# Tile 0's last column group as seven products of quarters, with a copy on VectorE, an earlier q packing and a later table load

## The chip, the cores and the metric

The kernel runs on one core of a Trainium2 chip. The core has five engines with a queue of instructions each: TensorE (PE in the profile; its weight loads are shown apart, as PEld), VectorE (DVE), ScalarE (ACT), GpSimd (POOL) and SyncE (SP). Every engine runs its own queue in order, and they meet through semaphores. Loads from main memory go over 16 DMA engines; nearly all of them are issued from POOL's queue here, the stores and the transposing DMAs from SP's.

The metric is the time of the kernel on the device, in microseconds (us), from the first instruction to the end. A profiled execution also has a span, from its first to its last recorded instruction.

## The reference

```python
def _attn_ref(q, k, v, g_norm):                      # (8, 8, 576, 64) each
    kv = np.einsum('bhsd,bhse->bhde', k, v)
    out = np.einsum('bhsd,bhde->bhse', q, kv)
    rms = np.sqrt(np.mean(out * out, axis=-1, keepdims=True) + 1e-06)
    return (out / rms * g_norm).astype(np.float32)

def _moe_ref(x, w_in, w_out):                        # (4608, 512), (512, 2048), (2048, 512)
    h = x @ w_in
    g = h * (1.0 / (1.0 + np.exp(-1.702 * h)))
    return (g @ w_out).astype(np.float32)
```

The attention's output, with its heads joined to rows of 512, is the second part's x.

## The kernel before

The 4608 rows are done in nine tiles of 512. Tile t (0 to 7) holds the first 512 rows of batch t; the ninth collects the 64 rows that are left over from each batch. For a tile the kernel needs the attention of its batch (transposed, as xT: four chunks `ko` of 128 model columns by 512 rows), then the "hidden" products (h = x @ w_in, as 16 column groups `fo` of 128), a gate on ScalarE (`gT`), and the projection with w_out.

Tiles 1 to 8 compute both matrix products with seven products of quarters instead of eight (Winograd's form of Strassen's scheme). For the hidden part, a group g (`PARTS` = 0, 2, 4, 6) covers columns i, i+1 and i+8, i+9. `SevenIn.product(p)` issues the four 256-wide matmuls of product p. The sums of weights (`ws`, made by `w_in_sums`) and of activations (`xS`, made by `Sums.form`) are made on VectorE. Products 1, 6, 7 and 4 accumulate one after another in one PSUM bank, "x". After product 1 that bank is copied to a bank "y", where product 2 adds to it (`snap[1]` names the engine, A for ScalarE, D for VectorE). Product 5 goes to a bank "z" and is copied to SBUF as `s5` (`snap[5]`). Once 5 and 6 are there, VectorE puts x + s5 into z, to which product 3 adds; after 7 it puts x + s5 into s5; 4 adds to x. The four results are gated from y, z, x and s5. So a product of the "x" bank may not start before VectorE has read what the one before it left there.

Tile 0 is done plainly: each column is four matmuls of 512 (`Hidden.mm`, line 487) and a gate (`Hidden.gate`, line 496). Columns 0 to 3 and 8, 9 run while batch 0's attention ends (lines 895 to 913); `first_columns` does the ten others in the order of `COLS`. Then `project_all` issues the 64 projection matmuls of tile 0 as steps n = 0 to 63: a row group `mo` (of four) and a column `fo` each. Between them, at step numbers given by hand, stand the units of batch 1's attention: `q` (transposes of q on TensorE, copied by ScalarE), `kv`, `out`, `ss` and `apply`. `at1(i, ...)` hangs a unit behind column i of `first_columns`, `at2(n, ...)` behind step n of the projection.

What VectorE does beside that in tile 0: it scales w_in by the norm's weights for the later tiles (`scale_w_in`, line 207; tile 0 has them in its x instead, and so uses w_in before it is scaled), makes the sums of w_in (lines 509 to 512) and of w_out (`weight_sum`, line 622), packs batch 1's q (`pack_q`, line 420), clears `kvd` (line 982), casts kv to `kvb` (line 385), and applies the roots (line 370).

The order on each engine is the order in which the Python code records it (`manual_schedule`); the framework adds the waits and hands out PSUM banks: `ps_a` and `ps_h` have three, `ps_o` has two.

Of the kernel before, what the change touches and what calls it, by code (L numbers as in the profile page):

```python
# [16 lines left out]
def kernel(  # L17
# [10 lines left out]
    nc = tc.nc  # L28

    B, H, S, D = q.shape  # L30
# [3 lines left out]
    FO = DFF // P  # L34
# [8 lines left out]
    PE_ = 96  # L43
    NJ = S // PE_
    GROUP = 6
    COLS = (0, 1, 2, 3, 8, 9, 10, 11, 4, 5, 6, 12, 13, 7, 14, 15)
    assert PE_ * NJ == S and PE_ % 32 == 0

    const = ctx.enter_context(tc.tile_pool(name="const", bufs=1))
# [15 lines left out]
    kvd = [const.tile([P, NPAIR, 2, 2, D], F16, name=f"kvd{i}") for i in range(2)]  # L65
# [15 lines left out]
    PARTS = range(0, HF, 2)  # L81
# [61 lines left out]
    for n in "kqv":  # L143
# [13 lines left out]
        out=ident,  # L157
# [340 lines left out]
    def quarters(w, f, k):  # L498

        hi = slice(HF * P + f.start, HF * P + f.stop)  # L500
        lower = slice(KH + k.start, KH + k.stop)
        return w[:, k, f], w[:, lower, f], w[:, k, hi], w[:, lower, hi]

    def w_in_sums(g0, g1):

        f = slice(2 * g0 * P, 2 * g1 * P)
        a11, a12, a21, a22 = quarters(w_in_sb, f, slice(0, KH))
        s = [ws[:, n, :, f] for n in range(4)]
        nc.vector.tensor_add(s[0], a21, a22)
        nc.vector.tensor_sub(s[1], s[0], a11)  # L510
        nc.vector.tensor_sub(s[2], a11, a21)
        nc.vector.tensor_sub(s[3], a12, s[1])

    class Sums:

# [27 lines left out]
    def copy(engine, to, src):  # L543
        (nc.vector.tensor_copy if engine == "D" else nc.scalar.copy)(to, src)  # L544
# [244 lines left out]
    def layers(t, units1, units2):  # L789
        hid = d0 if t == 0 else Hidden(t)  # L790
        seven = Seven(t, hid.gT) if t else None
        left = hid_seven(t, hid, seven, units1) if t else first_columns(hid, units1)
        osbs[t] = opool.tile([P, 4, DM], F32, name="osb", tag="osb")
        if t:
            todo = {n: [lambda x=x: seven.sums(*x) for x in xs] for n, xs in plan(t).later.items()}
            for n, us in units2.items():
                todo.setdefault(n, []).extend(us)
            for n, us in left.items():
                todo[n] = us + todo.get(n, [])
            seven.run(todo)  # L800
        else:
            project_all(hid.gT, units2)
        if t < B and t not in HALVED:
            store(t, 0, J)

    def first_columns(hid, units):

        for i, fo in enumerate(COLS):
            if i >= GROUP:
                for ko in range(KO):  # L810
                    hid.mm(ko, fo)
                hid.gate(fo)
            for u in units.get(i, ()):
                u()

    def project_all(gT, units):

        os = {}

        def project(mo, fo):  # L820
            if fo == 0:
                pool, tag = (ps_h, "hT") if mo < 2 else (ps_o, "o")
                os[mo] = pool.tile([P, DM], F32, name="o", tag=tag)
            nc.tensor.matmul(  # L824
                os[mo],
                gT[:, fo, mo * P : (mo + 1) * P],
                w_out_sb[:, fo, :],
                start=(fo == 0),
                stop=(fo == FO - 1),
            )  # L830
            if fo == FO - 1:
                copy = nc.scalar.copy if mo % 2 else nc.vector.tensor_copy
                copy(osbs[0][:, mo, :], os[mo])

        steps = [(mo, f + k) for f in (0, 4) for mo in range(4) for k in range(4)]
        steps += [(mo, f + k) for f in range(8, FO, 2) for mo in range(4) for k in range(2)]
        for n, (mo, fo) in enumerate(steps):
            project(mo, fo)
            for u in units.get(n, ()):
                u()  # L840

    def store(t, j0, j1):
        nc.sync.dma_start(
            out=out[t * S : t * S + SM, :].rearrange("(p j) m -> p j m", j=J)[:, j0:j1],
            in_=osbs[t][:, j0:j1],
        )
# [58 lines left out]
    for fo in range(4):  # L905
        d0.mm(2, fo)
    for fo in COLS[0:4]:
        d0.mm(KO - 1, fo)
        d0.gate(fo)
    for fo in COLS[4:GROUP]:  # L910
        for ko in range(KO):
# [13 lines left out]

    made = {}
    osbs = {}
    SECOND = Plan(
# [38 lines left out]
    def plan(t):  # L967
        return SECOND if t < EARLY else LATER if t < B - 1 else LAST_TWO

# [7 lines left out]
    for t in range(NT):  # L977
        b = t + 1
        u1, u2 = {}, {}

        def at1(i, f, *args):
            u1.setdefault(i, []).append(lambda: f(*args))

        def at2(i, f, *args):
            u2.setdefault(i, []).append(lambda: f(*args))  # L985

        def of(b, name, *args):
            return lambda: getattr(live[b], name)(*args)

        if t == 0:  # L990
            for l in range(2):
                at1(6, nc.vector.memset, kvd[l], 0.0)
            at1(7, scale_w_in, 0, 4)
            at1(7, w_in_sums, 0, 2)
            at1(8, start, 1)
            at1(12, scale_w_in, 4, 6)
            at1(12, w_in_sums, 2, 3)
            at1(13, load_q, 2)
            at2(4, nc.scalar.preload_act_table_set, "abs_reciprocal_sqrt_and_small")
            at2(18, weight_sum, 0, 0, HF)  # L1000
            at2(18, scale_w_in, 6, 8)
            at2(18, w_in_sums, 3, 4)
            for c in range(NPAIR):
                at1(12, of(1, "pack_q", c))
                at2(9 + 3 * c, of(1, "q", c))
                at2((38, 39, 51, 51)[c], of(1, "kv", c))
                at2((43, 45, 55, 56)[c], of(1, "out", c))
                at2((47, 50, 59, 61)[c], of(1, "ss", c))
                at2((49, 53, 59, 62)[c], of(1, "apply", c))
            for n in range(1, 4):  # L1010
                at2(19, weight_sum, n, 0, 2)
                at2(40, weight_sum, n, 2, 6)
            at2(39, load_kv, 2, 0, H // 2, False)
            at2(51, clear_rest)
            at2(51, load_kv, 2, H // 2, H)

            def first_sum():
                made[1] = Sums(1, xT[1])
                made[1].form(0)

            at2(55, first_sum)
        elif b < B:
            todo = plan(t)
            at1(todo.steps.index("kv"), of(b, "kv_all", todo.keep))
            if t == 1:
                at1(5, start, b)
                at1(5, of(b, "transpose_q"))
                at1(4, nc.scalar.preload_act_table_set, "gelu_apprx_sigmoid_and_others")
                for n, i in ((1, 8), (2, 11), (3, 16)):
                    at1(i, weight_sum, n, 6, HF)  # L1030
            if t + 2 < B:
                late = max(15, todo.steps.index("kv") + 1)
                at1(late, load_kv, t + 2)
                at1(late, load_q, t + 2)
                at2(100, start, t + 2)
                at2(100, of(t + 2, "transpose_q"))
            if t == B - 2:
                for early in range(EARLY):
                    at1(20, load_q_rest, early, qre[early])
                at2(100, rests.transpose)  # L1040
            at = todo.attn
            at2(at["table"], nc.scalar.preload_act_table_set, "abs_reciprocal_sqrt_and_small")
            for h in range(2):
                at2(at["roots"][h], of(b, "roots", h))
            for j in range(J):
                for name in ("rows", "add_up", "turn"):
                    at2(at[name][j], of(b, name, j))
            at2(46, of(b, "out", NPAIR))
            at2(74, of(b, "ss", NPAIR))
            at2(80, of(b, "apply", NPAIR))  # L1050
            at2(82, nc.scalar.preload_act_table_set, "gelu_apprx_sigmoid_and_others")
        elif t < B:
            at2(16, rests.out)
            at2(34, nc.scalar.preload_act_table_set, "abs_reciprocal_sqrt_and_small")
            at2(44, rests.ss)
            at2(50, rests.apply)
            at2(52, nc.scalar.preload_act_table_set, "gelu_apprx_sigmoid_and_others")
        layers(t, u1, u2)


# [28 lines left out]
```

## Time and profile before

| | us |
|---|---|
| three runs | 261.21, 263.64, 263.35 |
| their median | 263.35 |
| the profiled execution | 261.35 |
| its span | 259.6 |

The page of the profile gives, for each engine, its busy time, share of the span and number of instructions. A line of an instruction group names the line of the kernel, the engine, the operation, the tile written and the tiles read with their shapes, how often it ran; after the bar busy time and mean ns of one; after the second bar the idle time in front of them and what ended it. In a timeline a line begins with start and duration in us, and ends, in square brackets, with the engine's idle time before it and who released it. Matmuls overlap in the array: a matmul's busy time is longer than the distance from its start to the next one's.

### The profile page before, as it was taken

What the parts mean: (1) busy time and instruction counts of PE and PEld (TensorE: products, weight loads), DVE (VectorE), ACT (ScalarE), POOL (GpSimd) and SP (SyncE); (2) the same over time, 40 slices, a digit from 0 to 9 for tenths busy, and PEclk for the clock granted to TensorE, in tenths of its full rate; (3) what the DMA queues carried; (4) which work ended last, traced back from release to release, by engine and by line L of the source; (5) the groups of instructions that cost most, each with busy time, mean ns of one, the idle gap of its engine ahead of it and who ended that gap; (6) DMA issues with size and microseconds to landing.
All of it is one profiled execution on the core that took longest, in us unless ns stands there. A gap on an engine that the chain in (4) does not pass through costs nothing.

```text
span 259.6 us, 6081 instructions
## 1 busy us (share of the span) xinstructions
PE 252.1 (97%) x2475; PEld 205.9 (79%) x2475; DVE 194.2 (75%) x350; ACT 174.1 (67%) x313; POOL 56.3 (22%) x85
## 2 busy tenths in 40 slices
PE   8899999999999999999999999999999999999992
PEld 2434544788888988899889888988899889888882
DVE  1656658999968986898689968995899578467931
ACT  2487715988649964996499649964897569737810
POOL 8962335116034003500250017200000000000000
PEclk9999999999999999999999999999999999999999
DMA  8999999999999976994799969998601520021005
GB/s 171 186 202 204 203 203 196 246 162 154 179 166 139 225 107 162 159 204 68 169 65 222 148 159 130 232 99 144 153 3 27 149 91 3 0 110 54 4 0 162
DMA packets 69886, 35.42 MB, mean 136 GB/s; under 512 B 39330, under 2 KB 67746, under 8 KB 69602
## 3 DMA queue, kind: packets, MB, share of 16 engines
q0 software_dynamic: 39056, 18.19, 56.2%
q1 hardware_dynamic: 30480, 16.45, 29.6%
q8 instruction: 19, 0.31, 0.5%
q10 hardware_dynamic: 322, 0.39, 0.5%
q14 instruction: 9, 0.07, 0.1%
HBM read 36.70 MB, written 9.44 MB: 178 GB/s over the span
## 4 chain that ended last, share of the span: by engine, by line
PE 92%; POOL 3%; DMA 2%; ACT 1%; DVE 1%; issue 0%
PE h L594 38%; PE o L716 38%; PE o L824 5%; PE hT L487 5%; DMA w_in_sb<-in_moe_w_in_dram 2%; PE outR L308 2%; PE kvp L236 2%; POOL qraw L99 1%; PE ss L356 1%; POOL kraw L101 1%; POOL vbuf L101 1%; ACT rs L358 1%; PE kvp L248 0%; PE outT L281 0%; PE q L429 0%; DVE xT L366 0%
## 5 line engine op out<-in xcount | busy, mean ns | idle before, releaser
L574 ACT ACTIVATE gT<-h 128x512 f16<-128x512 f32 x96 | 52.8, 604 | 5.4 <-PE h L594 5.4
L594 PEld LDWEIGHTS <-ws 128*128 128x128 f16 x512 | 50.1, 98 | 6.0
L716 PEld LDWEIGHTS <-gS 128*128 128x128 f16 x512 | 49.7, 98 | 5.8
L594 PE MATMUL h<-xS,ws 128*128 128x256 f16 x384 | 52.2, 273 | 0.0
L716 PE MATMUL o<-tw,gS 128*128 128x256 f16 x384 | 46.4, 273 | 0.0
L594 PEld LDWEIGHTS <-w_in_sb 128*128 128x128 f16 x384 | 37.1, 98 | 4.8
L716 PEld LDWEIGHTS <-gT 128*128 128x128 f16 x384 | 37.0, 98 | 4.0
L716 PE MATMUL o<-w_out_sb,gT 128*128 128x256 f16 x256 | 33.5, 273 | 0.0
L594 PE MATMUL h<-xT,w_in_sb 128*128 128x256 f16 x224 | 31.9, 273 | 0.0
L691 DVE TENSOR_TENSOR osb<-o,qf 128x512 f32<-128x512 f32 (+1 forms) x25 | 16.7, 668 | 14.7 <-PE o L716 11.9
L608 DVE TENSOR_TENSOR h<-h,s 128x512 f32<-128x512 f32 x32 | 22.2, 697 | 6.7 <-PE h L594 5.5
L113 POOL DMA_DIRECT2D kraw<-in_k_dram x7 | 6.0, 854 | 92.7 <-PE kvp L236 87.4
L610 DVE TENSOR_TENSOR s<-h,s 128x512 f32<-128x512 f32 x32 | 22.1, 691 | 4.1 <-PE h L594 3.3
L646 DVE TENSOR_TENSOR gS<-gT 128x512 f16<-128x512 f16 (+2 forms) x32 | 21.6, 684 | 0.6 <-ACT gT L574 0.6
L574 ACT ACTIVATE gT<-s 128x512 f16<-128x512 f32 x32 | 19.8, 628 | 2.6 <-DVE s L610 2.6
L985 ACT ACT_TABLE_LOAD x15 | 19.2, 1283 | 0.3
L745 POOL DMA_DIRECT2D out_dram<-osb x2 | 1.1, 559 | 84.3 <-DVE osb L691 84.3
L358 ACT ACTIVATE rs<-ss,eps_t 128x512 f32<-128x512 f32 (+1 forms) x14 | 8.2, 597 | 16.0 <-PE ss L356 15.9
L594 PE MATMUL h<-xS,w_in_sb 128*128 128x256 f16 x128 | 18.9, 273 | 0.0
L544 ACT COPY h<-h 128x512 f32<-128x512 f32 x27 | 15.7, 587 | 2.1 <-PE h L594 2.0
L594 PE MATMUL h<-xT,ws 128*128 128x256 f16 x112 | 16.8, 273 | 0.0
L544 ACT COPY s<-h 128x512 f32<-128x512 f32 x18 | 10.6, 589 | 8.8 <-PE h L594 8.2
(105 smaller groups left out, 373.3 us busy)
## 6 DMA issues: line engine op xcount, KB each, us to landing
out_dram<-osb SPq DMA_DIRECT2D x12, 512.0 KB, 3.0
kraw<-in_k_dram POOLq DMA_DIRECT2D x5, 512.0 KB, 8.2
vbuf<-in_v_dram POOLq DMA_DIRECT2D x5, 512.0 KB, 11.8
qraw<-in_q_dram POOLq DMA_DIRECT2D x4, 512.0 KB, 14.4
out_dram<-osb SPq DMA_DIRECT2D x2, 1024.0 KB, 5.6
qbuf<-in_q_dram POOLq DMA_DIRECT2D x3, 512.0 KB, 12.8
w_in_sb<-in_moe_w_in_dram POOLq DMA_DIRECT2D x2, 512.0 KB, 10.5
w_out_sb<-in_moe_w_out_dram POOLq DMA_DIRECT2D x2, 512.0 KB, 14.8
```

Source lines behind the costliest of these rows:

```text
L358: nc.scalar.activation(rs[:, 0:n], t[:, 0:n], AFT.Abs_reciprocal_sqrt, bias=eps_t, scale=1.0 / D)
L487: nc.tensor.matmul(self.h[fo], w_in_sb[:, ko, fo * P : (fo + 1) * P], self.x[:, ko], start=(ko == 0), stop=(ko == KO - 1),)
L544: (nc.vector.tensor_copy if engine == "D" else nc.scalar.copy)(to, src)
L574: nc.scalar.activation(self.gT[:, to, n * TH : (n + 1) * TH], src, AFT.Gelu_apprx_sigmoid)
L594: nc.tensor.matmul(bank[name][:, a], w, x, start=(p in (1, 5) and a == 0 and k == 0), stop=(k == KH - 1), skip_group_check=True,)
L608: nc.vector.tensor_add(bank["z"], bank["x"], self.s5)
L610: nc.vector.tensor_add(self.s5, bank["x"], self.s5)
L646: op(s[:, n, lo], a, b)
L691: nc.vector.tensor_add(o, ps, self.kept[with_][:, m])
L716: nc.tensor.matmul(o, a, w, start=(p in (1, 2, 5) and i == 0 and (mo == 0 or split)), stop=(i == HF - 1), skip_group_check=True,)
L824: nc.tensor.matmul(os[mo], gT[:, fo, mo * P : (mo + 1) * P], w_out_sb[:, fo, :], start=(fo == 0), stop=(fo == FO - 1),)
L985: u2.setdefault(i, []).append(lambda: f(*args))
```

## The change

Columns 6, 7, 14 and 15 of tile 0 (group 3) are computed with the seven products. `COLS` keeps the six early columns, and `COLS_LATER` lists the others, in which a string is a product: column 10, 11, 4, product 1, column 5, product 2, columns 12 and 13, products 5, 6 and 7. Products 3 and 4 stand in the projection, behind steps 3 and 7. The plan `FIRST` says that product 1 is copied by ScalarE and product 5 by VectorE. The sums of x are made behind column 10, group 3's sums of the unscaled w_in behind column 13; behind step 19 of the projection that part of w_in is scaled and summed again for the later tiles.

Beside it, the first scaling and the sums of w_in move to other places, `kvd` is cleared by GpSimd, the packing of q hangs behind step 0 of the projection and not behind column 13, with the q load for tile 2 behind step 8, and ScalarE's table of roots is loaded behind step 20, not step 4. The attention's units from `kv` on stand one or two steps later, both units of a kv pair at one step, and the last eight projection steps go through the row groups in the order 2, 0, 3, 1.

```diff
-    COLS = (0, 1, 2, 3, 8, 9, 10, 11, 4, 5, 6, 12, 13, 7, 14, 15)
+    COLS = (0, 1, 2, 3, 8, 9)
+    COLS_LATER = (10, 11, 4, "1", 5, "2", 12, 13, "5", "6", "7")
...
-    def w_in_sums(g0, g1):
+    def w_in_sums(g0, g1, which=range(4)):
...
         else:
+            for n, us in left.items():
+                units2[n] = us + units2.get(n, [])
             project_all(hid.gT, units2)
...
     def first_columns(hid, units):
 
-        for i, fo in enumerate(COLS):
-            if i >= GROUP:
+
+        xs = Sums(0, hid.x)
+        part = SevenIn(hid, xs, len(PARTS) - 1, FIRST)
+        gates = []
+        for i, fo in enumerate(COLS_LATER):
+            if isinstance(fo, str):
+                gate = part.product(int(fo))
+                if gate:
+                    gates.append(gate)
+            else:
                 for ko in range(KO):
                     hid.mm(ko, fo)
                 hid.gate(fo)
+            if fo == 5 or fo == 12:
+                while gates:
+                    gates.pop()()
+            if i == 0:
+                for n in range(4):
+                    xs.form(n)
             for u in units.get(i, ()):
                 u()
+
+        def late(p):
+            gates.append(part.product(p))
+            gates.pop()()
+            while p == 4 and gates:
+                gates.pop()()
+
+        return {3: [lambda: late(3)], 7: [lambda: late(4)]}
...
             if fo == FO - 1:
-                copy = nc.scalar.copy if mo % 2 else nc.vector.tensor_copy
+                copy = nc.vector.tensor_copy if mo in (2, 0) else nc.scalar.copy
                 copy(osbs[0][:, mo, :], os[mo])
 
         steps = [(mo, f + k) for f in (0, 4) for mo in range(4) for k in range(4)]
-        steps += [(mo, f + k) for f in range(8, FO, 2) for mo in range(4) for k in range(2)]
+        steps += [(mo, f + k) for f in (8, 10, 12) for mo in range(4) for k in range(2)]
+        steps += [(mo, 14 + k) for mo in (2, 0, 3, 1) for k in range(2)]
...
+    FIRST = Plan("", {}, {}, {1: "AAAA", 5: "DDDD"}, "D", "aaaa", "aaaa", {}, ())
...
             for l in range(2):
-                at1(6, nc.vector.memset, kvd[l], 0.0)
-            at1(7, scale_w_in, 0, 4)
-            at1(7, w_in_sums, 0, 2)
-            at1(8, start, 1)
-            at1(12, scale_w_in, 4, 6)
-            at1(12, w_in_sums, 2, 3)
-            at1(13, load_q, 2)
-            at2(4, nc.scalar.preload_act_table_set, "abs_reciprocal_sqrt_and_small")
+                at1(0, nc.gpsimd.memset, kvd[l], 0.0)
+            at1(1, scale_w_in, 0, 4)
+            at1(1, w_in_sums, 0, 2, (0, 1))
+            at1(2, start, 1)
+            at1(7, w_in_sums, 3, 4)
+            at2(1, w_in_sums, 0, 2, (2, 3))
+            at2(8, scale_w_in, 4, 6)
+            at2(8, w_in_sums, 2, 3)
+            at2(8, load_q, 2)
+            at2(20, nc.scalar.preload_act_table_set, "abs_reciprocal_sqrt_and_small")
             at2(18, weight_sum, 0, 0, HF)
-            at2(18, scale_w_in, 6, 8)
-            at2(18, w_in_sums, 3, 4)
+            at2(19, scale_w_in, 6, 8)
+            at2(19, w_in_sums, 3, 4)
             for c in range(NPAIR):
-                at1(12, of(1, "pack_q", c))
+                at2(0, of(1, "pack_q", c))
                 at2(9 + 3 * c, of(1, "q", c))
-                at2((38, 39, 51, 51)[c], of(1, "kv", c))
-                at2((43, 45, 55, 56)[c], of(1, "out", c))
-                at2((47, 50, 59, 61)[c], of(1, "ss", c))
-                at2((49, 53, 59, 62)[c], of(1, "apply", c))
+                at2((39, 39, 53, 53)[c], of(1, "kv", c))
+                at2((44, 46, 56, 57)[c], of(1, "out", c))
+                at2((48, 51, 60, 62)[c], of(1, "ss", c))
+                at2((50, 54, 60, 63)[c], of(1, "apply", c))
...
             at2(39, load_kv, 2, 0, H // 2, False)
-            at2(51, clear_rest)
-            at2(51, load_kv, 2, H // 2, H)
+            at2(53, clear_rest)
+            at2(53, load_kv, 2, H // 2, H)
```

More of the change, by code (lines that the diff above doesn't have):

```diff
@@ L508, in w_in_sums @@
         s = [ws[:, n, :, f] for n in range(4)]
[L509 to L512, printed above, removed]
+        for n in which:
+            op, a, b = (
+                (nc.vector.tensor_add, a21, a22),
+                (nc.vector.tensor_sub, s[0], a11),
+                (nc.vector.tensor_sub, a11, a21),
+                (nc.vector.tensor_sub, a12, s[1]),
+            )[n]
+            op(s[n], a, b)
     class Sums:
```

## The prediction

> **What bounds the kernel now.** I read the busy table first, then the chain of waits, then a table of stages.
>
> ```profile
> PE 252.1 (97%) x2475; PEld 205.9 (79%) x2475; DVE 194.2 (75%) x350; ACT 174.1 (67%) x313; POOL 56.3 (22%) x85
> PE 92%; POOL 3%; DMA 2%; ACT 1%; DVE 1%; issue 0%
> 17.00:28.27 11.27, 11.22 (x52) 5.07 (x52) 7.59 (x14) 8.94 (x16) 3.51 (x5) 1.00 1.30 204
> 28.27:46.60 18.33, 18.18 (x137) 8.75 (x136) 11.63 (x28) 9.08 (x15) 7.93 (x11) 1.00 1.35 200
> 46.60:73.50 26.90, 26.90 (x288) 23.69 (x287) 24.85 (x45) 20.70 (x37) 5.26 (x7) 1.00 1.24 178
> ```
>
> TensorE (PE) is busy 97% of the span and carries 92% of the chain that ended last. The last three rows are tile 0's columns, tile 0's projection (with batch 1's attention), and tile 1; columns are length, then busy time of PE, weight loads, VectorE (DVE), ScalarE (ACT), GpSimd (POOL), the granted clock (1.00), DMA. PE has no pause in tile 1, so a microsecond won or lost in tile 0 reaches the end whole. Busy hides short stalls behind modelled tails; I therefore work with start times.
>
> **The columns: less work, two new waits.**
>
> ```profile
> 17.05 11.38 PE L487 MATMUL hT<-xT,w_in_sb 128*128 128x512 f16 x52 [0.27 <-DVE xT L366]
> 28.27 2.32 PE L824 MATMUL o<-w_out_sb,gT 128*128 128x512 f16 x10
> 75.12 11.02 PE h L594 x100
> L594 PEld LDWEIGHTS <-ws 128*128 128x128 f16 x512 | 50.1, 98 | 6.0
> ```
>
> From the first row's start to the second's, 52 matmuls of 512 columns take 11.22, so 0.2158 each. The third (the chain in order of time) gives 0.110 for one of 256. The change drops four columns, 16 x 0.2158 = 3.45, and adds 28 x 0.110 = 3.08: 0.37 us less PE work. The weight loads, 98 ns in the fourth row, still fit under 110.
>
> [...]
>
> What a product waits for:
>
> ```profile
> 17.53 3.77 ACT L496 ACTIVATE gT<-hT 128x512 f16<-128x512 f32 x7
> 22.43 0.60 ACT L496 ACTIVATE gT<-hT 128x512 f16<-128x512 f32 x1 [0.27 <-PE hT L487]
> 47.43 0.61 ACT L544 COPY h<-h 128x512 f32<-128x512 f32 x1
> 21.57 0.87 DVE L207 TENSOR_SCALAR w_in_sb<-w_in_sb,g_col 128x2048 f16<-128x2048 f16 x1 [2.70 <-PE hT L487]
> 22.48 0.69 DVE L509 TENSOR_TENSOR ws<-w_in_sb 128x1024 f16<-128x1024 f16 x1
> 23.81 0.68 DVE L511 TENSOR_TENSOR ws<-w_in_sb 128x1024 f16<-128x1024 f16 x1
> 23.83 0.72 POOL L195 DMA_DIRECT2D w_out_sb<-in_moe_w_out_dram  x1 [1.88 <-DMA w_in_sb<-in_moe_w_in_dram]
> 26.41 0.42 DVE L509 TENSOR_TENSOR ws<-w_in_sb 128x512 f16<-128x512 f16 x1
> ...
> 27.54 0.42 DVE L512 TENSOR_TENSOR ws<-w_in_sb,ws 128x512 f16<-128x512 f16 x1
> 49.14 0.69 DVE L544 COPY s<-h 128x512 f32<-128x512 f32 x1
> L608 DVE TENSOR_TENSOR h<-h,s 128x512 f32<-128x512 f32 x32 | 22.2, 697 | 6.7 <-PE h L594 5.5
> ```
>
> Column 10 starts at 17.05 + 12 x 0.2158 = 19.64, before and after. Then 10, 11 and 4 end issuing at 22.23, "1" at 22.67, column 5 at 23.53. "2" adds into a bank that ACT copies from "1". ACT gates column 4 from 22.43 and, at its pitch of 0.54 (3.77 for seven), copies from about 22.97 for 0.61: PE waits until about 23.63, 0.1 lost. "2" ends at 24.07; the weights of columns 12 to 15 have landed by 23.83, where POOL's issue was released by them; 12 and 13 end at 25.80. "5" needs the first w_in sum of the group. DVE's scaling still waits for column 11 and two sums follow as in the rows, so the new 0.42 sums start near 23.85 and the first is ready near 24.3: hidden. The four x sums (0.42 each) sit in DVE's 2.70 of waiting.
>
> The third wait is not hidden. "5" ends at 26.24, "6" at 26.68, and "7" accumulates into the very bank that DVE must still read for z = x + s5 (the add behind "6"); that add needs the copy s5 of "5". A 512 matmul shows 0.38 busy at 0.216 spacing, so results stand about 0.16 after issue ends: 26.40. DVE copies 26.45 to 27.14 (0.69), adds to about 27.87 (0.70 by the last row), and "7" starts at 27.90 instead of 26.68: 1.22 us of idle PE, with the whole projection queued behind it. In tile 1 other products stand between these three; here nothing does. "7" ends at 28.34, where the projection began at 28.27. "3" and "4" follow inside the projection, 0.88 together; the second add (done near 29.25) comes before "4" at 30.5. So step 8 starts at 30.95, against 28.27 + 8 x 0.2158 = 30.00. Sum: -0.37 + 0.10 + 1.22 = +0.95.
>
> **Moves beside PE.**
>
> ```profile
> 28.73 1.03 DVE L420 COPY qbuf<-qraw 128x512 f16<-128x512 f16 x4 [0.77 <-DMA qraw<-in_q_dram]
> 31.33 1.23 DVE L622 TENSOR_TENSOR tw<-w_out_sb 128x2048 f16<-128x2048 f16 x1 [1.58 <-DMA w_out_sb<-in_moe_w_out_dram]
> 32.47 0.87 DVE L207 TENSOR_SCALAR w_in_sb<-w_in_sb,g_col 128x1024 f16<-128x1024 f16 x2
> 38.73 0.59 DVE L385 CAST kvb<-kvp 64x128 f16<-64x128 f32 x2 [2.79 <-PE kvp L248]
> 39.91 1.24 ACT L299 ACTIVATE sq<-outT 128x512 f16<-128x512 f32 x2 [5.86 <-PE outT L281]
> 17.06 1.02 DVE L982 MEMSET kvd<- 128x512 uint32 x2
> 1.26 0.20 POOL L165 MEMSET ones<- 128x128 f16 x1
> 33.25 0.91 POOL L131 DMA_DIRECT2D qraw<-in_q_dram  x1 [1.02 <-DVE w_in_sb L207]
> 48.38 6.38 SPq L271 DMA_TRANSPOSE qTd<-qraw  x1
> 59.64 0.39 PE L308 MATMUL outR<-kvd,qTd 128*128 128x128 f16 x4
> ```
>
> The packing of q, though recorded sooner, now stands behind the second add and starts at about 29.25, not 28.73; its first reader, q's transpose after step 9, comes near 31.2: nothing. DVE's queue up to the kvb casts is then packing 1.03, two sums of 0.69, two scalings of pairs 0.87, eight small w_in sums at 0.39 (the four from 26.41 to 27.96; the group's sums are made twice now, unscaled and scaled), 1.23, and three weight sums of that size: 9.7 us, to 38.95. The casts come due at 38.73 + 0.95 - 0.15 = 39.5. Nothing, but 0.6 is all that covers it. The table load (one, behind the last gate and the four q copies, by 36) lies in ACT's 5.86 of idle. The memsets move to POOL, in front of tile 2's q load (33.25) with its two rest loads and the kv loads behind it. No row shows POOL clearing such a tile: DVE's 1.02 for both is the lower bound, and POOL's 0.20 for an eighth as many columns, times sixteen, 3.2, the upper; I take 2, between them. The q load feeds SP's transpose at 48.38, first read at 59.64; 2 us vanish there.
>
> **The projection's end.**
>
> ```profile
> 40.78 0.38 PE L356 MATMUL ss<-sq,ones 128*128 128x512 f16 x1
> 41.20 0.69 ACT L358 ACTIVATE rs<-ss,eps_t 128x512 f32<-128x512 f32 x1
> 41.94 0.38 PE L356 MATMUL ss<-sq,ones 128*128 128x512 f16 x1
> 42.46 0.57 PE L248 MATMUL kvp<-vbuf,kraw 96*64 96x64 f16 x24
> 42.96 1.04 PE L824 MATMUL o<-w_out_sb,gT 128*128 128x512 f16 x4
> 43.84 0.38 PE L281 MATMUL outT<-qT,kvb 128*128 128x512 f16 x1
> 45.13 0.38 PE L356 MATMUL ss<-sq,ones 128*128 128x512 f16 x1
> 45.97 0.38 PE L356 MATMUL ss<-sq,ones 128*128 128x512 f16 x1
> 46.61 0.60 PE L594 MATMUL h<-xT,w_in_sb 128*128 128x256 f16 x4
> ```
>
> The attention units sit one or two steps later. The two kv groups become one run and save about 0.15. The second kv pair leaves three steps (0.65) instead of four (0.86) before the product that needs its cast, which can start 0.88 after kv's last matmul was issued (42.96 to 43.84): 0.2 lost. The last ss goes into the bank of the one before; it waits for that root: from ss to ss 0.38 + 0.04 + 0.69 + 0.05 = 1.16, as between the first two before (40.78 to 41.94), where 45.13 to 45.97 was 0.84. That is 0.3 lost. Together +0.35; bounds -0.4 (every present pause gone) and +0.7.
>
> Total +1.3. The profiled execution took 261.35 us (span 259.6 and 1.75 around it) and would take 262.65; the median of the runs, 263.35, is 2.0 above it and becomes **264.6**.
>
> **Rivals.** First, product 7's wait is no wait of consequence, because DVE answers faster or PE's order hides it, and the saved 0.37 stands together with up to 0.4 of removed pauses: 262.6 to 263.0, faster. For: the work does fall. Against: the 0.69 and 0.70 rows, and nothing queued between.
>
> Second, slower by more than 1%: DVE becomes late at the kvb casts. Its place is the queue priced at 9.7 us with 0.6 of cover; POOL's clearing runs in the same stretch as DVE's scalings and sums. What DVE loses there beyond 0.6 us, PE waits for at the casts; 2 us lost gives 1.3 + 1.4 = 2.7, hence 266.0, and from 1.9 on it passes 1%. For: the 2.79 of idle ahead of the casts is used up. Against: the packing alone can slip freely. [...]
>
> Third, weight loads set the pace of the seven products. If a product matmul cost 0.123 (3.45 / 28) nothing would be saved: 265.0. Against it: 100 of them at 0.110.
>
> **Numbers.** Chances: forecast 0.68, first rival 0.12, second 0.14, third 0.03, the rest 0.03. A measurement of this kernel tells about 1% from no change. The forecast (+0.5%) and the first rival lie within 1%; the second is beyond. So slower 0.16, same 0.80, faster 0.04, the last for runs that fall near 261.2 on one side and 263.6 on the other, as the three shown do. The range: from 262.65, the sum on the profiled execution, less 0.65 for the tail's lower bound, 262.0; to the highest run, 263.64 + 1.3 + 0.85 for the tail's upper bound and POOL, 265.8.
>
> **What would show it.** Right: a pause of about 1.2 us before the third group of "h" products from xS in tile 0, with DVE's copy and add in it back to back; step 8 about 0.95 later; tile 1 starting near 47.9. Wrong: that pause under 0.5; kvb casts that start with no wait for PE (DVE late); or tile 1 starting before 46.6.

## The result, and the profile after

| | kernel before | changed kernel |
|---|---|---|
| median of 22 runs each, us | 261.68 | 262.52 |
| lowest and highest, us | 261.21, 263.64 | 262.16, 262.94 |
| the profiled execution, us | 261.35 | 262.91 |
| its span, us | 259.6 | 261.1 |

The ratio of the changed kernel to the one before is 1.0027 (95% interval 1.0016 to 1.0038): 0.7 us slower by the ratio, 0.84 by the medians. The forecast was 264.6 us, or 1.3 us slower than a base of 263.35; the range of 262.0 to 265.8 holds the time. The direction is right, the size is not, and the base is off by more than the change. Of 85 further runs of the kernel before, made beside the experiments, the three above 263 us had a mean granted clock of 0.989 and the other 82 one of 0.995 to 1.000; for 263.64 and 263.35 no clock is on record.

The page of the changed kernel: busy time of PE and the others, the engines' shares of the chain, and the group of products with a sum as operand (after the second bar the idle time in front of them).

```profile
PE 251.7 (96%) x2487; PEld 206.9 (79%) x2487; DVE 198.1 (76%) x359; ACT 174.2 (67%) x314; POOL 58.7 (22%) x87
...
PE 90%; POOL 3%; DMA 3%; DVE 1%; ACT 1%; issue 0%; DVEq 0%
...
L599 PE MATMUL h<-xS,ws 128*128 128x256 f16 x396 | 53.9, 273 | 1.2 <-DVE h L613 1.2
```

PE has 12 matmuls more and 0.4 us less busy time, yet the span is 1.5 longer. The group that had no idle time before now has 1.2 us of it in one place, ended by VectorE's addition. The stages of the changed kernel, cut at the same times as those of before (length, then busy time of PE, weight loads, DVE, ACT, POOL, the granted clock, DMA):

```profile
17.00:28.27 11.27, 9.88 (x52) 4.99 (x52) 7.13 (x15) 8.22 (x15) 3.87 (x5) 1.00 1.30 204
28.27:46.60 18.33, 18.04 (x143) 9.28 (x143) 14.74 (x35) 8.51 (x14) 8.80 (x12) 1.00 1.35 200
46.60:73.50 26.90, 26.56 (x280) 22.90 (x278) 25.25 (x47) 22.23 (x40) 6.33 (x9) 1.00 1.24 174
```

The clock is 1.00 as before. The first pauses stand in the columns: 11.27 - 9.88 = 1.39 us without PE, where it was 0.05. The timeline of that place:

```profile
18.40 4.49 PE L488 MATMUL hT<-xT,w_in_sb 128*128 128x512 f16 x20 [0.22 <-DMA w_in_sb<-in_moe_w_in_dram]
...
26.22 1.04 PE L599 MATMUL h<-xS,ws 128*128 128x256 f16 x8
26.86 0.69 DVE L549 COPY s<-h 128x512 f32<-128x512 f32 x1 [1.03 <-PE h L599]
27.68 0.70 DVE L613 TENSOR_TENSOR h<-h,s 128x512 f32<-128x512 f32 x1
28.44 0.60 PE L599 MATMUL h<-xS,ws 128*128 128x256 f16 x4 [1.18 <-DVE h L613]
31.47 0.59 PE L853 MATMUL o<-w_out_sb,gT 128*128 128x512 f16 x2
```

The row at 26.22 is products 5 and 6, together 8 x 0.110 = 0.88 of issue, to 27.10. Then VectorE copies, adds, and product 7 starts at 28.44: 1.34 us in which PE issues nothing, with copy and add back to back. (The row counts 1.18 of idle: the eight matmuls' busy time of 1.04 reaches 0.16 past their 0.88 of issue.) The first row belongs to this execution alone: a matmul waited for a transfer of w_in. A second profile of the same kernel, in the experiments, doesn't have that wait, and is compared with the kernel before here:

```profile
22.37 0.60 PE L599 MATMUL h<-xT,w_in_sb 128*128 128x256 f16 x4
...
28.08 0.60 PE L599 MATMUL h<-xS,ws 128*128 128x256 f16 x4 [1.18 <-DVE h L613]
31.11 0.59 PE L853 MATMUL o<-w_out_sb,gT 128*128 128x512 f16 x2
...
47.50 0.38 PE L357 MATMUL ss<-sq,ones 128*128 128x512 f16 x1 [0.34 <-ACT rs L359]
47.93 0.60 PE L599 MATMUL h<-xT,w_in_sb 128*128 128x256 f16 x4
```

Product 1 starts at 22.37; the 24 matmuls of 0.2158 in front of it put the start of that row at 17.19, where the kernel before has 17.05. From there step 8 of the projection (31.11) is 13.92 away; before, it was 30.00 - 17.05 = 12.95. From step 8 to tile 1 (47.93) it is 16.82, before 46.61 - 30.00 = 16.61. So the columns and the two late products cost 0.97 us, and the rest of the projection 0.21. What tile 1 does with it is in the chain of waits, in order of time. The kernel before:

```profile
46.78 9.44 PE h L594 x84
56.21 0.75 PE kvp L236 x40
```

and the changed kernel's second profile:

```profile
48.10 9.17 PE h L599 x84
57.27 0.75 PE kvp L237 x40
```

The same 84 matmuls take 9.17 and not 9.44: tile 1 gives back 0.27. Together 0.97 + 0.21 - 0.27 = 0.91, and 0.14 for the start; the two profiled executions are 262.45 - 261.35 = 1.10 apart. Where the 0.27 was in the kernel before, its timeline shows:

```profile
46.97 0.59 ACT L833 COPY osb<-o 128x512 f32<-128x512 f32 x1
47.05 0.60 PE L594 MATMUL h<-xS,ws 128*128 128x256 f16 x4
...
47.61 0.60 PE L594 MATMUL h<-xT,w_in_sb 128*128 128x256 f16 x4
...
50.25 0.60 PE L594 MATMUL h<-xT,w_in_sb 128*128 128x256 f16 x4
50.81 1.03 PE L594 MATMUL h<-xS,ws 128*128 128x256 f16 x8
```

Four matmuls take 0.44 from start to start; here it is twice 0.56. PE counted as busy through both, since the modelled end of a matmul (0.60 after the group's start) covers the gap. The group at 47.61 starts 0.05 after ScalarE has ended a copy of an accumulator (46.97 + 0.59 = 47.56). That this copy held it back is a reading, on which one of the experiments below rests.

### The profile page after: what moved, and what is told of

The parts are those of the page before. It is cut to its first block, busy times and chain, and to the rows that moved or that the text cites. A ratio compares the mean times of both kernels' runs of the same rounds, so it can differ in the third digit from the quotient of the medians.

```text
span 261.1 us, 6119 instructions
## 1 busy us (share of the span) xinstructions
PE 251.7 (96%) x2487; PEld 206.9 (79%) x2487; DVE 198.1 (76%) x359; ACT 174.2 (67%) x314; POOL 58.7 (22%) x87
## 3 DMA queue, kind: packets, MB, share of 16 engines
HBM read 36.70 MB, written 9.44 MB: 177 GB/s over the span
## 4 chain that ended last, share of the span: by engine, by line
PE 90%; POOL 3%; DMA 3%; DVE 1%; ACT 1%; issue 0%; DVEq 0%
PE h L599 39%; PE o L721 37%; PE o L853 5%; DMA w_in_sb<-in_moe_w_in_dram 3%; PE hT L488 3%; PE outR L309 2%; PE kvp L237 2%; POOL qraw L100 1%; POOL kraw L102 1%; POOL vbuf L102 1%; PE ss L357 1%; POOL w_in_sb L171 1%; ACT rs L359 1%; PE kvp L249 0%; PE outT L282 0%; PE q L430 0%
## 5 line engine op out<-in xcount | busy, mean ns | idle before, releaser
L579 ACT ACTIVATE gT<-h 128x512 f16<-128x512 f32 x99 | 54.5, 604 | 9.3 <-PE h L599 9.3
L599 PEld LDWEIGHTS <-ws 128*128 128x128 f16 x528 | 51.7, 98 | 7.7 <-issue 1.4
L599 PE MATMUL h<-xS,ws 128*128 128x256 f16 x396 | 53.9, 273 | 1.2 <-DVE h L613 1.2
L599 PEld LDWEIGHTS <-w_in_sb 128*128 128x128 f16 x396 | 38.3, 98 | 5.5 <-issue 0.2
L599 PE MATMUL h<-xT,w_in_sb 128*128 128x256 f16 x232 | 33.1, 273 | 0.0
L613 DVE TENSOR_TENSOR h<-h,s 128x512 f32<-128x512 f32 x33 | 23.0, 698 | 6.9 <-PE h L599 5.5
L615 DVE TENSOR_TENSOR s<-h,s 128x512 f32<-128x512 f32 x33 | 22.8, 691 | 4.8 <-PE h L599 4.0
L579 ACT ACTIVATE gT<-s 128x512 f16<-128x512 f32 x33 | 20.5, 628 | 2.5 <-DVE s L615 2.5
L599 PE MATMUL h<-xS,w_in_sb 128*128 128x256 f16 x132 | 19.5, 273 | 0.0
L853 PE MATMUL o<-w_out_sb,gT 128*128 128x512 f16 x64 | 16.6, 379 | 0.0
```

The source lines that it names most:

```text
L579: nc.scalar.activation(self.gT[:, to, n * TH : (n + 1) * TH], src, AFT.Gelu_apprx_sigmoid)
L599: nc.tensor.matmul(bank[name][:, a], w, x, start=(p in (1, 5) and a == 0 and k == 0), stop=(k == KH - 1), skip_group_check=True,)
L613: nc.vector.tensor_add(bank["z"], bank["x"], self.s5)
L615: nc.vector.tensor_add(self.s5, bank["x"], self.s5)
L853: nc.tensor.matmul(os[mo], gT[:, fo, mo * P : (mo + 1) * P], w_out_sb[:, fo, :], start=(fo == 0), stop=(fo == FO - 1),)
```

## Experiments

Each was compared with the kernel before, in runs on the same chip. Ratios are to the kernel before.

### Column 13 between products 6 and 7

```diff
-    COLS_LATER = (10, 11, 4, "1", 5, "2", 12, 13, "5", "6", "7")
+    COLS_LATER = (10, 11, 4, "1", 5, "2", 12, "5", "6", 13, "7")
...
-            at1(7, w_in_sums, 3, 4)
+            at1(6, w_in_sums, 3, 4)
```

> Column 13 stands between products 6 and 7, with group 3's w_in sums one column earlier; the work is that of the changed kernel. Theory (product 7 waits for VectorE's copy and add, 1.35 us of idle in the changed kernel's profile): 0.86 of that is covered by the column, about 0.45 stays, and the time falls by 0.9 us from the changed kernel's, to about that of the kernel before (261.7). Rival (the loss sits in the end of the projection or in the moved loads and clears): the time stays at 262.5.

Median 261.46 us against 261.51 (12 and 32 runs), ratio 1.0000 (0.9987 to 1.0013). Product 7 in the timeline:

```profile
26.85 0.60 PE L599 MATMUL h<-xS,ws 128*128 128x256 f16 x4 [0.32 <-DVE h L613]
27.29 1.03 PE L853 MATMUL o<-w_out_sb,gT 128*128 128x512 f16 x4
```

Four matmuls of other work take 0.86 us out of the pause, the idle time falls from 1.18 to 0.32, and the changed kernel's loss is gone. Beside the kernel before, the same products with the same copies cost no time that can be measured once something stands between them.

### Product 7 behind step 5 of the projection

```diff
-    COLS_LATER = (10, 11, 4, "1", 5, "2", 12, 13, "5", "6", "7")
+    COLS_LATER = (10, 11, 4, "1", 5, "2", 12, 13, "5", "6")
...
-        return {3: [lambda: late(3)], 7: [lambda: late(4)]}
+        def seven():
+            gates.insert(0, part.product(7))
+
+        return {5: [seven], 7: [lambda: late(3)], 13: [lambda: late(4)]}
```

The sums of w_in that stood behind the projection's steps 1 and 8 follow at step 9.

> Product 7 stands behind step 5 of the projection, 3 behind step 7, 4 behind step 13, and two sums of w_in that stood ahead of the second add on VectorE behind step 9. Theory: six steps (1.30 us) lie between 6 and 7, so no wait is left, the saved 0.37 us of TensorE work shows, and the time is 1.2 to 1.3 us below the changed kernel's, 0.3 to 0.4 below the kernel before. Rival: no change from 262.5.

Median 261.45 against 261.51, ratio 1.0009 (0.9986 to 1.0031), with two of 12 runs above 263. Two lines of the timeline around product 7, and one at tile 1's start:

```profile
26.61 1.46 PE L856 MATMUL o<-w_out_sb,gT 128*128 128x512 f16 x6
...
27.95 0.60 PE L599 MATMUL h<-xS,ws 128*128 128x256 f16 x4
...
46.51 0.60 PE L599 MATMUL h<-xT,w_in_sb 128*128 128x256 f16 x4
```

No wait is left before product 7, and tile 1 starts 0.10 before that of the kernel before, with 9.17 us for its 84 matmuls. The median is 1.07 below the changed kernel's 262.52, not the 1.2 to 1.3 expected. A gain over the kernel before of some tenths, which the landmarks suggest, isn't shown by the times.

### The changed kernel with the end of before

`kv`, `out`, `ss` and `apply` at the due times of before, with the clearing and the load behind step 51 and not 53, and the last steps through the row groups 0 to 3 as before. "Due times" below means all of these steps.

```diff
-                at2((48, 51, 60, 62)[c], of(1, "ss", c))
+                at2((47, 50, 59, 61)[c], of(1, "ss", c))
...
-        steps += [(mo, f + k) for f in (8, 10, 12) for mo in range(4) for k in range(2)]
-        steps += [(mo, 14 + k) for mo in (2, 0, 3, 1) for k in range(2)]
+        steps += [(mo, f + k) for f in range(8, FO, 2) for mo in range(4) for k in range(2)]
```

> The changed kernel with the projection's end of the kernel before (steps of the attention's units, order of the last eight steps). By the prediction's term (the new end costs 0.35 us, all of it reaching the end) the time falls by 0.35 from the changed kernel's. By the reading of the two traces (the new end costs 0.2 at the start of tile 1, but tile 1's first products then run 0.27 faster) it stays within 0.1 of the changed kernel's 262.5.

Median 262.76 against 261.51, ratio 1.0045 (1.0029 to 1.0060). That is no better than the changed kernel. Tile 1 starts at 47.48 for 47.93, of which 0.25 is an earlier start of the columns (16.94 for 17.19), and the chain has its 84 matmuls at 9.44 again. What the old end wins in front of tile 1, 0.20, tile 1 gives away again.

### The end of after in the kernel before

The reverse of the last one: sixteen columns, and only the due times and the order of the last steps from the change.

> The kernel before with only the changed end of the projection. By the prediction's term 0.35 us slower than the kernel before. By the reading of the traces the start of tile 1 comes 0.2 later and its first 84 product matmuls take 9.17 us and not 9.44, so within 0.1 of the kernel before.

Median 261.70 against 261.51, ratio 1.0010 (0.9991 to 1.0028).

```profile
46.31 0.38 PE L356 MATMUL ss<-sq,ones 128*128 128x512 f16 x1 [0.34 <-ACT rs L358]
...
46.74 0.60 PE L594 MATMUL h<-xT,w_in_sb 128*128 128x256 f16 x4
```

The last sum of squares now waits for the root of the one before, as predicted, and tile 1 starts later (46.74 for 46.61; from the columns' start, which is 16.97 here, 0.21 later). It doesn't reach the end: kvp of tile 1 starts at 56.00 in this profile's timeline and at 56.14 in that of before, 39.03 and 39.09 from the columns' start.

### The order of the last steps alone

```diff
-        steps += [(mo, f + k) for f in range(8, FO, 2) for mo in range(4) for k in range(2)]
+        steps += [(mo, f + k) for f in (8, 10, 12) for mo in range(4) for k in range(2)]
+        steps += [(mo, 14 + k) for mo in (2, 0, 3, 1) for k in range(2)]
```

> The kernel before with one part of the changed end: the projection's last two steps of the four accumulators in the order 2, 0, 3, 1, and every due time as before. Theory (it is this order that lets ScalarE be done earlier with its copies, and so takes the pauses out of tile 1's first products, while the due times cost the 0.2 at tile 1's start): tile 1's 84 products take 9.17 us for 9.44, tile 1 starts within 0.15 of before, and the median is 0.1 to 0.4 below it. Rival (the order and the due times belong together): no gain, or the last sum of squares waits for a root as in the changed kernel, and the median is that of the kernel before within 0.1.

Median 261.61 against 261.65, ratio 1.0001 (0.9988 to 1.0014). The theory fell in one half. In the timeline, and in the chain of waits:

```profile
28.59 2.32 PE L824 MATMUL o<-w_out_sb,gT 128*128 128x512 f16 x10
...
46.60 0.38 PE L356 MATMUL ss<-sq,ones 128*128 128x512 f16 x1 [0.34 <-ACT rs L358]
...
47.25 0.60 PE L594 MATMUL h<-xT,w_in_sb 128*128 128x256 f16 x4
```

```profile
47.41 9.17 PE h L594 x84
```

From the projection's start to tile 1's it is 18.66 us, 0.32 more than before (46.61 - 28.27 = 18.34), and the wait for the root is there, so the order is enough to make that wait, without the new due times. The same order makes tile 1's products run without the two gaps. One edit moves a stall of 0.3 from behind a boundary to a place in front of it, and the sum is nothing.

### The changed kernel once more

No edit.

> The changed kernel as it is, once more, to part what belongs to the change from what belonged to its one profiled execution. Theory of the wait (product 7 waits for VectorE's copy and add; its profiled execution also lost 0.49 us where columns 8 and 10 met a late transfer): a median 0.7 to 1.0 us above the kernel before, a pause of 1.2 to 1.4 us before product 7, and the late transfer gone, so that tile 1 starts near 47.8 and not at 48.29. Rival (the late transfer comes from the moved instructions): tile 1 again near 48.3, and column 8 waits for w_in's transfer again.

Median 262.45 against 261.61 (5 and 23 runs), ratio 1.0037 (1.0025 to 1.0049): 0.84 us again by the medians. Its profile is the second one shown above; the late transfer is gone, and tile 1 starts at 47.93.

### Product 5 copied twice

```diff
                 copy(self.snap[5], self.s5, bank["z"])
+                if self.first:
+                    copy(self.snap[5], self.s5, bank["z"])
```

`first` is true for tile 0's plan alone.

> The changed kernel with VectorE's copy of product 5 in tile 0 issued twice in a row, so that the add behind it, and product 7, come one copy (0.69 us) later. Theory of the wait: PE's pause before product 7 grows from 1.2-1.4 to about 2.0 us, tile 1 starts 0.7 later than in the changed kernel, and the median is 0.7 us above it, 1.4 to 1.7 above the kernel before. Rival (the pause is refilled later, because PE waits again for VectorE's kvb casts or ScalarE's roots): under 0.3 us above the changed kernel.

Median 263.31, ratio 1.0073 (1.0061 to 1.0085), 0.86 above the changed kernel in the same runs.

```profile
28.87 0.60 PE L600 MATMUL h<-xS,ws 128*128 128x256 f16 x4 [1.90 <-DVE h L616]
...
48.73 0.60 PE L600 MATMUL h<-xT,w_in_sb 128*128 128x256 f16 x4
```

The idle time grows by 0.72, one copy, and tile 1 starts 0.80 later, 0.07 of it because the columns start at 17.26 and not at 17.19. Nothing behind the pause absorbs it.

### Product 5 copied by ScalarE

```diff
-    FIRST = Plan("", {}, {}, {1: "AAAA", 5: "DDDD"}, "D", "aaaa", "aaaa", {}, ())
+    FIRST = Plan("", {}, {}, {1: "AAAA", 5: "AAAA"}, "D", "aaaa", "aaaa", {}, ())
```

> The changed kernel with the copy of product 5 in tile 0 on ScalarE instead of VectorE. Theory of the wait (what matters is when the add behind the copy ends): ScalarE still has column 13's gate to finish, so its copy ends 0.1 to 0.3 us later than VectorE's, the pause before product 7 is as long or longer, and the median is 0 to 0.3 us above the changed kernel, 0.8 to 1.2 above the kernel before. Rival (it is VectorE's queue that is late): the pause shrinks by half a microsecond or more and the median comes to within 0.5 of the kernel before.

Median 262.33 against 261.65, ratio 1.0026 (1.0006 to 1.0046): as the changed kernel.

```profile
26.69 0.60 ACT L549 COPY s<-h 128x512 f32<-128x512 f32 x1
...
27.33 0.70 DVE L613 TENSOR_TENSOR h<-h,s 128x512 f32<-128x512 f32 x1 [1.76 <-ACT s L549]
28.08 0.60 PE L599 MATMUL h<-xS,ws 128*128 128x256 f16 x4 [1.14 <-DVE h L613]
```

ScalarE copies faster (0.60 for 0.69) but starts later, behind a gate (26.69; VectorE in the second profile 26.50). The add starts at the same time (27.33 and 27.32). So the pause isn't a late queue of VectorE's: with either engine, copy, add and product follow one another.

### The moves alone

The kernel before with `kvd` cleared by GpSimd, q packing at step 0, the q load at step 8 and the table at step 20.

```diff
-                at1(6, nc.vector.memset, kvd[l], 0.0)
+                at1(0, nc.gpsimd.memset, kvd[l], 0.0)
...
-            at1(13, load_q, 2)
-            at2(4, nc.scalar.preload_act_table_set, "abs_reciprocal_sqrt_and_small")
+            at2(8, load_q, 2)
+            at2(20, nc.scalar.preload_act_table_set, "abs_reciprocal_sqrt_and_small")
...
-                at1(12, of(1, "pack_q", c))
+                at2(0, of(1, "pack_q", c))
```

> The kernel before with the moves alone: kvd's memsets on GpSimd at the front, q packing at the projection's step 0, q's load at its step 8, ScalarE's table at its step 20; the sixteen columns and the projection's end as before. Theory of the prediction (the moves lie beside PE): ratio 1.000, within 0.3 us, tile 1 starting at 46.6 as before. Rival (VectorE or GpSimd delays the kvb casts, or the table meets ScalarE's square): 0.3 us or more above the kernel before, with a wait of PE for DVE or ACT in the projection's second half.

Median 261.69 against 261.61, ratio 1.0006 (0.9990 to 1.0021): nothing, as forecast. Tile 1 starts 29.57 us after the columns do, before 29.56. But the timeline has something that the forecast knew only as a rival:

```profile
32.39 1.85 POOL L982 MEMSET kvd<- 128x1024 f16 x2
32.59 2.72 DVE L207 TENSOR_SCALAR w_in_sb<-w_in_sb,g_col 128x1024 f16<-128x1024 f16 x2
...
39.02 0.28 DVE L385 CAST kvb<-kvp 64x128 f16<-64x128 f32 x1 [1.12 <-PE kvp L248]
```

Two scalings that take 0.87 in the kernel before take 2.72 here. The first began 0.20 after the first memset and took 1.93 for 0.48; it ended at 34.52, after the second memset (32.39 + 1.85 = 34.24). The second took 0.87 for 0.48, while GpSimd issued q's load (34.17 to 35.08); what held it isn't settled, as such a pair beside that issue took 1.12 in the changed kernel's second profile and 0.87 in the run with ScalarE's copy. It costs nothing, because VectorE still stands idle for 1.12 us in front of the casts.

### Product 7 later, with the end of before

> Product 7 behind the projection's step 5, and the projection's end as in the kernel before: so the seven products and the moves alone, with no wait left. Theory (the products save 0.37 us, tile 1's first products wait for ScalarE's copies of the projection as in the kernel before): tile 1 starts near 46.2 for 46.6, its 84 products take 9.4 us, and the median is 0.2 to 0.5 us below the kernel before. Rival (the saving of the products isn't there, or tile 1 gives it back): within 0.1 us of the kernel before.

Median 261.65, that of the kernel before in the same runs; ratio 1.0005 (0.9990 to 1.0020). The rival holds, and the timeline says why:

```profile
29.46 1.03 DVE L421 COPY qbuf<-qraw 128x512 f16<-128x512 f16 x4 [1.18 <-DMA qraw<-in_q_dram]
...
38.69 1.04 PE L856 MATMUL o<-w_out_sb,gT 128*128 128x512 f16 x4
...
39.25 0.58 DVE L386 CAST kvb<-kvp 64x128 f16<-64x128 f32 x2
39.89 0.39 PE L282 MATMUL outT<-qT,kvb 128*128 128x512 f16 x1 [0.17 <-DVE kvb L386]
```

The casts start without having waited for PE: VectorE is late. Four matmuls from 38.69 end at 39.55, and the product that needs the cast starts at 39.89, 0.34 late. That takes back nearly all of the 0.37 that the seven products save. VectorE packs q from 29.46, when its load is there, and has no pause from then to the casts, 9.79 us later; the second add of the products stands in that queue too. Tile 1 starts at 47.02, not near 46.2: the columns start 0.21 later here than in the kernel before, and their first 24 matmuls take 0.18 longer in this execution.

### Product 7 later, the last order, the due times of before

> Product 7 behind the projection's step 5, the last steps in the order 2, 0, 3, 1, and the due times of the kernel before. Theory (0.37 from the products and 0.27 from tile 1's first products, with nothing lost at the end): the median 0.4 to 0.7 us below the kernel before, tile 1 starting near 46.2 with 84 products of 9.17 us. Rival (one of the two isn't to be had together with the old due times): 0 to 0.3 below.

Median 261.65, ratio 1.0000 (0.9989 to 1.0010). The rival again.

```profile
39.61 0.39 PE L282 MATMUL outT<-qT,kvb 128*128 128x512 f16 x1 [0.18 <-DVE kvb L386]
```

VectorE is late at the casts here too (0.35); tile 1 starts at 47.06, not near 46.2, its 84 matmuls take 9.17, and the last sum of squares waits 0.34 for the root.

### Product 7 later, one sum of squares a step earlier

The kernel with product 7 behind step 5 and the end of after, but

```diff
-                at2((48, 51, 60, 62)[c], of(1, "ss", c))
+                at2((48, 51, 59, 62)[c], of(1, "ss", c))
```

> Product 7 behind the projection's step 5, as in the run of that name, and the sum of squares of pair 2 one step earlier (59 for 60), so that one product of the projection lies between the root and the last sum of squares that waits for it. Theory (the last sum waits 0.34 us for the root of the one before, and a fifth of a microsecond of it is cover that one product gives): PE's pause before the last sum falls from 0.34 to about 0.12, tile 1 starts 0.2 earlier than in the run with product 7 later alone, and 0.3 before that of the kernel before; the median 0.2 to 0.5 us below the kernel before. Rival (tile 1 gives such tenths back, as it did with the old end): tile 1 starts earlier, but its 84 products of the chain take 9.4 us for 9.17, and the median is that of the kernel before within 0.2.

Median 261.29 against 261.61 (12 and 23 runs), ratio 0.9994 (0.9983 to 1.0004). Part of the step is there. (The profiled execution is a long one, 262.37 us; its columns start at 18.60, so only distances are read here.)

```profile
46.46 0.81 PE L856 MATMUL o<-w_out_sb,gT 128*128 128x512 f16 x3
...
47.40 0.38 PE L357 MATMUL ss<-sq,ones 128*128 128x512 f16 x1
```

Three matmuls from 46.46 end issuing at 47.11, and the last sum starts 0.29 behind them; with two, in the run without this edit, it was 45.15 + 0.43 = 45.58 to 46.08, or 0.50. The expected 0.2 is there in the profile. The medians lie as expected and the interval holds 1, so a gain isn't shown. It is the lowest median of all twelve, and the lower end of its interval, 0.9983, is 0.44 us below the kernel before.

## Why the prediction was right in direction and wrong in size

**The base: "the median of the runs, 263.35, is 2.0 above it and becomes 264.6".** This step failed. Two of the three runs shown lay above 263. Of the 22 runs of the comparison only those two did, and of the 85 beside the experiments three, at the lower clock that the section on the result gives; the medians there were 261.51 to 261.65. Had the sum been made on the profiled execution (261.35, as the prediction itself worked out: 262.65), the forecast would have been 0.13 off. Of the 2.08 us between 264.6 and 262.52, 263.35 - 261.68 = 1.67 is the base. (The range has a slip as well: from +0.35 to the tail's own bound of -0.4 is 0.75, and not the 0.65 that was taken off.)

**"PE has no pause in tile 1, so a microsecond won or lost in tile 0 reaches the end whole."** This step failed for the projection's end. The stage showed PE busy for 26.90 of 26.90 us and still held 0.27 of gaps. The prediction says that busy time hides short stalls and used starts in tile 0, but not in tile 1. For the columns the sentence holds: with the copy doubled, 0.72 more of wait came out as 0.86 in the median.

**The projection's end, "together +0.35".** Mis-sized: at tile 1's start it was +0.21, and with tile 1's 0.27 it was -0.06. Its three parts in the second profile: the kv groups in one run save 0.22 (taken as 0.15), the second pair's three steps for four lose 0.1 (taken as 0.2), and the wait of the last sum for the root loses 0.31 (taken as 0.3). The run with the order alone showed that this order also takes the gaps out of tile 1, which the prediction didn't look for. Both runs that change the end alone show no difference that can be measured.

**The columns, "Sum: -0.37 + 0.10 + 1.22 = +0.95".** Right: 0.97. The pause before product 7 is 1.34 for 1.22, product 2's wait 0.04 for 0.10 (22.80 + 4 x 0.2158 = 23.66, started at 23.70 in the second profile). Two runs that fill the pause with other work take the loss away, one that lengthens it adds to it, and one that hands the copy to the other engine leaves it. So the cause is shown, and the first rival (a wait of no consequence) is out.

**The moves beside PE, "nothing".** Right, and the run with four of them alone (the clearing, the packing, the load and the table) shows it; the moved sums of w_in weren't run by themselves. GpSimd's clearing takes 1.85 for an assumed 2. The cover at the kvb casts was put at 0.6 and is 1.11 in the first profile, whose rows these are, and 0.93 in the second:

```profile
31.82 0.87 DVE L208 TENSOR_SCALAR w_in_sb<-w_in_sb,g_col 128x1024 f16<-128x1024 f16 x2
...
32.96 1.85 POOL L1013 MEMSET kvd<- 128x1024 f16 x2
...
39.97 0.59 DVE L386 CAST kvb<-kvp 64x128 f16<-64x128 f32 x2 [1.11 <-PE kvp L249]
```

**The second rival, VectorE late at the casts.** It didn't happen in the changed kernel, but it is nearer than a cover of 0.93 to 1.11 says. The pause before product 7 is part of that cover: in the two runs without the pause and with the old due times PE waited 0.34 and 0.35 for VectorE. With product 7 later and the new due times the casts also start without a wait (38.50), and only the fifth projection step in front of the product hides it. The kernel before had 2.79 us of idle time there: the seven products' own work on VectorE, and the scaling and sums of w_in that moved into the projection, have used it up. And the memset began 0.27 us after the scalings had ended; in the run with the moves alone they met, and VectorE's two scalings took 1.85 longer, more than the cover. The 2 us of the rival's sum were an assumption; no row of before shows such a loss. A changed kernel in which they meet wasn't tried.

**Third rival, weight loads as the pace.** Out: the columns' sum comes out with 0.110 a matmul, and tile 1's groups of four stand 0.44 apart.

What stays open is whether the seven products are worth anything here at all. Their 0.37 is in the sum of the columns, and in no run did it show as a time below the kernel before that its interval tells from none.

## What to carry to other kernels

Products that accumulate in one bank with a copy and an add between them need other work of that length (here 1.3 us) between them. Where such a group stood alone at the end of a stage, the pause was paid in full (1.34 us); one column in between left 0.48 of it, and six projection steps left none. The sums, copies and adds load VectorE (its idle time ahead of the casts fell from 2.79 to 1.11 and 0.93 us), so its next deadline has to be looked at as well. A stage whose busy time equals its length may still hold gaps (tile 1 before: 0.27 us in 26.90): look at the distance from start to start before saying that a change ahead of it passes through whole. And a small change (0.3% here) needs a base of many runs, with the granted clock of each beside it: the median of three was 1.67 us off, twice the change itself.

## What the runs showed of the hardware

A scaling on VectorE that came behind a GpSimd memset took longer: begun 0.20 us after the first of two memsets, it took 1.93 us for 0.48 and ended, at 34.52, only after both, which ended at 34.24 (the run with the moves alone). Where the scaling was ahead and the memset came second, each pair took only 0.12 longer, as in the run with product 7 later (0.99 for 0.87, and 1.97 for 1.85):

```profile
31.45 0.99 DVE L208 TENSOR_SCALAR w_in_sb<-w_in_sb,g_col 128x1024 f16<-128x1024 f16 x2
...
32.26 1.97 POOL L1016 MEMSET kvd<- 128x1024 f16 x2
```

With product 5 copied twice only the memsets did (2.00). VectorE's additions beside the same memset kept their time in the changed kernel (0.43 and 0.42 us for 512 columns, before 0.42). Why the scaling behind the memsets took 1.45 us longer, and the pairs that came first 0.12, these runs don't show.

The granted clock of one profiled execution, that of the run with one sum of squares a step earlier (mean 0.990, 262.37 us for a median of 261.29), fell early on. The page gives it in tenths for 40 slices of 6.5 us, here from the start:

```profile
PEclk9979999999999999999999999999999999999998
```

In the third slice (13.0 to 19.5 us) it is 7 tenths, where the pages of the kernel before and of the changed kernel have 9, and the columns start at 18.60, 1.54 later than in the run with product 7 later alone (17.06). The three runs of the kernel before at 0.989 weren't profiled, so where they lost their time isn't shown.
